# Row maxima of an attention block: transposed by 4-byte DMA loads instead of a TensorE matmul, and joined at the head of a step

## The chip, the cores and the metric

The kernel runs on one core of one Trainium2 chip. The metric is the device time of one execution in microseconds (us); the median of several runs counts. Five engines work side by side, each through its own queue in order: TensorE (PE, whose weight loads are listed apart as PEld), VectorE (DVE), ScalarE (ACT), GpSimd (POOL) and SyncE (SP), which issues most of the transfers. They meet through semaphores.

## The reference

A pre-normalized attention block with 32 heads of 16 dimensions over 2048 tokens, gated by the SiLU of a dense block with GELU:

```python
xn = _layernorm(x, axis=-1)                       # x: 1 x 2048 x 512
# attention, H = 32 heads, Dh = 16
scores = jnp.einsum("bhqd,bhkd->bhqk", q, k) * (Dh ** -0.5)
p = _softmax(scores, axis=-1)
o = jnp.einsum("bhqk,bhkd->bhqd", p, v)           # then @ wo
# dense block: 512 -> 1376 -> 512
h = _gelu(jnp.einsum("bsd,df->bsf", xn, w1) + b1)
g = _silu(jnp.einsum("bsf,fd->bsd", h, w2) + b2)
return x + s * g                                  # s: the attention's output
```

Everything is float32; the matmuls work on pairs of a rounded high part and a low rest. The weights are scaled up (factor 8), so the softmax needs its row maxima subtracted.

## The kernel before

**Units.** Attention is cut into 32 units. Unit `u` is a group of 4 heads (`g = u // 4`) and a chunk of 512 queries (`c = u % 4`). Each unit is gone through twice:
- *maxima* ("S"): 64 score tiles of 128 queries x 512 keys, which serve only to find each query's largest score. `s_mm` (L184) makes a tile in one of three banks, and `s_max` (L190) reduces it on DVE to two partial maxima per query in the tile `mx`. Two heads sit in the two 64-row halves of TensorE (`a` = 0, 1), two more behind each other (`p` = 0, 1).
- *attention*: in 16 steps of 128 keys each, four transposed score tiles of 128 keys x 512 queries ("T", `t_one`, L716), the exponential on ACT (L718), and the PV matmuls of the step before ("V", `pv_step`, L781).

**The maxima's way.** The subtraction is part of the T matmul: `QT[u]`, the queries of a unit, has two extra rows in each half (48 and 49) with the high and the low part of the negated maximum, against two rows of ones beside the keys. So the maxima, which arise one query to a partition, are needed as rows, one query to a column. Before, this goes in four parts. `s_end0` joins the 8 partial maxima of each query to `nm` (128 x 16, L248), behind the next S tile's reduction, and has POOL split them into `nmh` (L251, L252). `s_end1` transposes `nmh` by a matmul with the identity (L268), for two units at once up to unit 27 (`PAIRED`), into a bank of the S ring (stage one, and the last unit) or of the T ring. `s_end2` copies the result to `mh` (ACT in stage one, L276; DVE later, L278) and stores it in `mh_d` (L279). `load_mh` fetches two rows of a half in one transfer, two transfers a unit (L152). `later` counts ticks (four a step) until the transposition may be issued, and `need` is the first step at which `load_mh` may stand.

**Stages.** In stage one (to about 470 us) layer norm, the projections and the dense block run, and the first 576 S tiles (9 units, `LEAD`) are interleaved by `fill`. From then on come 512 attention steps, 16 a unit, their order written out by hand in `ORDER` and `AFTER`: with 3 S tiles (S, or X and Y for a tile in two halves), 4 T tiles and V a step until step 491, and with the output projection's half-array matmuls (`w_halves`, L905) afterwards. A short tail ends it. Small jobs (loads, divisions, gates) hang on steps in `todo`.

**Queues around the change.** SP issues, for each unit, the denominator's gather and four moves of the output (`o_move`, L801, L804), six query loads for attention (`load_qt`, L135), the maxima (`load_mh`), the denominators' store and broadcast load (`o_den`, L810, L813), and six query loads for the maxima of the unit after next (`load_qs`, L135, called at the end of `s_end0`). Near the end it also issues the gate's loads (`load_gx`, L837, L838). POOL issues the key loads of later groups (`load_k`, L110) and does the divisions (`o_div`, L819).

Of the kernel before, what the change touches and what calls it, by code (L numbers as in the profile page):

```python
# [8 lines left out]
F32 = mybir.dt.float32  # L9
# [7 lines left out]
P = 128  # L17
# [6 lines left out]
CH = 512  # L24
# [17 lines left out]
HC = CH // 2  # L42
PAIRED = 28
KB = 3
# [5 lines left out]
def fused(ctx: ExitStack, tc: tile.TileContext, x, wqk, wv, wo, w1, b1, w2, b2, out):  # L50
# [34 lines left out]

    QS, QT, MX, NM, MH = {}, {}, {}, {}, {}
    SYNC = mybir.DependencyInfo(mybir.DependencyClass.Sync, mybir.DependencyReason.DATA)
# [61 lines left out]
    def load_mh(u):  # L149
        assert u in sent  # L150
        for a in range(2):
            nc.sync.dma_start(QT[u][64 * a + 48:64 * a + 50].bitcast(F32), mh_d[u, :, a::2, :])  # L152

# [3 lines left out]
    later, ended, errands, sent = [], [], [], set()  # L157

    def units_of(u):
        return (u,) if u >= PAIRED else (u - u % 2, u - u % 2 + 1)  # L160

# [45 lines left out]

    jobs, whole, cut, put_off = [], [], [], []

    def s_op(op):  # L210
# [6 lines left out]
        elif op == "X":  # L217
# [4 lines left out]
            cut[2:] = [ps, pool, x]  # L222
            run_off()
        else:
# [9 lines left out]

    def run_off():
        while put_off:
            put_off.pop(0)()

    def s_end0(u):
        nm = qring.tile([P, GH * NCH], F32, name="nm")  # L240
        n = len(units_of(u))
        if u == units_of(u)[0]:
            NM[u] = qring.tile([P, 2, 2, GH * NCH], F32R, name="nmh")[:, :n]
        hl = NM[units_of(u)[0]][:, u % n]
        if u == units_of(u)[-1]:
            later.append([12 if "seen" in prog else 8, units_of(u)[0]])
        mx = MX.pop(u).rearrange("p a b c n -> p (a b) (c n)")
        nc.vector.tensor_reduce(nm, mx, axis=AX.X, op=OP.max, negate=True)  # L248

        def two():  # L250
            nc.gpsimd.tensor_copy(hl[:, 0], nm)  # L251
            nc.gpsimd.tensor_sub(hl[:, 1], nm, hl[:, 0].bitcast(F32))  # L252

        put_off.append(two)
        if "seen" in prog or u == NU - 1:
            run_off()
        del QS[u]
        if "seen" in prog:
            ask_qs(u + 2)
        else:  # L260
            load_qs(u + 2)

    prog = {}

    def s_end1(u):
        pm = s_tile()[0] if "seen" in prog or u == NU - 1 else t_tile()
        n = 2 * GH * NCH * len(units_of(u))
        nc.tensor.matmul(pm[:n, :P], NM.pop(u).rearrange("p u i a -> p (u i a)"), ident_r, start=True, stop=True)  # L268
        MH[u] = pm

    def s_end2(u):
        us = units_of(u)
        n = 2 * GH * NCH * len(us)
        mh = qring.tile([4 * GH * NCH, P], F32, name="mh", bufs=1)
        if "seen" in prog:
            nc.scalar.activation(mh[:n], MH.pop(u)[:n, :P], AF.Copy)  # L276
        else:
            nc.vector.tensor_copy(mh[:n], MH.pop(u)[:n, :P])  # L278
        nc.sync.dma_start(mh_d[us[0]:us[-1] + 1].rearrange("u i j (q s) -> (u i j q) s", s=P), mh[:n])  # L279
        sent.update(us)  # L280

# [277 lines left out]
    writer = {}  # L559
    s_when, put, row = [], [0], [0, 0]  # L560
    ndown = sum(1 for e in plan if e[0] == "down")
    ROWS = 12 * (4 * VQ + 2 * len(pairs)) + 6 * ndown - 10 + 2 * LEAD - 2 * (LEAD // 32) - FILL0

    def fill(a):
        due = FILL0 + put[0] + sum(made) * ROWS // (4 * LEAD)
        if sum(made) < 4 * LEAD and row[a] >= due and (made[0] <= made[1]) == (a == 0):
            taken()
            if later and later[0][0] <= 0:
                put[0] += 2
                u = later.pop(0)[1]  # L570
                s_end1(u)
                s_end2(u)
                return
            s_one(a)
            row[a] += 1
            tick()
# [357 lines left out]
    for u in range(NU):  # L934
# [116 lines left out]
```

## Time and profile before

| | us |
|---|---|
| median of 3 runs | 1572.92 (1572.62 to 1572.99) |
| the profiled execution | 1573.31 |
| its span | 1571.4 |
| S reductions on DVE, 2048 (L190) | 1298.8 busy |
| exponentials on ACT, 1533 + 515 (L718) | 826.0 + 310.9 busy |
| PV matmuls, 4096 (L781) | 545.3 busy |
| joining reductions, 32 (L248) | 8.8 busy |
| POOL's two parts of the split, 32 each (L251, L252) | 6.3 and 7.1 busy |

The profile is one execution, seen by the chip's profiler. A group row gives the line, the engine, the operation, tiles, count and durations (minimum / median / maximum in ns in the view of one tile or line). A timeline row gives start and length in us, engine, line, operation and, in square brackets, the idle time just before it with what ended it. A row of stages gives, for each engine, its busy time in the stage and its instructions. In the view of the transfers, a line of 40 digits is the mean busy share of the 16 DMA engines in 40 equal slices of the window, in tenths, and the row of a queue gives its packets, megabytes and the share of the 16 engines' time that they took. Tiles `slot`, `kt`, `qt` and `pst` are buffers that different stages share.

### The profile page before, as it was taken

What the parts mean: (1) busy time and instruction counts of PE and PEld (TensorE: products, weight loads), DVE (VectorE), ACT (ScalarE), POOL (GpSimd) and SP (SyncE); (2) the same over time, 40 slices, a digit from 0 to 9 for tenths busy, and PEclk for the clock granted to TensorE, in tenths of its full rate; (3) what the DMA queues carried; (4) which work ended last, traced back from release to release, by engine and by line L of the source; (5) the groups of instructions that cost most, each with busy time, mean ns of one, the idle gap of its engine ahead of it and who ended that gap; (6) DMA issues with size and microseconds to landing.
All of it is one profiled execution on the core that took longest, in us unless ns stands there. A gap on an engine that the chain in (4) does not pass through costs nothing.

```text
span 1571.4 us, 31849 instructions
## 1 busy us (share of the span) xinstructions
PE 1564.2 (100%) x12264; PEld 952.0 (61%) x12264; DVE 1397.1 (89%) x2290; ACT 1233.8 (79%) x2397; POOL 371.9 (24%) x394
## 2 busy tenths in 40 slices
PE   9999999999999999999999999999999999999998
PEld 7899999999994444444444444444444444444455
DVE  7599898989988999999999999999999999999834
ACT  4333333333339999999999999999999999999984
POOL 4145575766741001001100100100010000000143
PEclk9999999999999999999999999999999999999999
DMA  6626343454322114111511511321061111110163
GB/s 208 152 59 150 122 139 99 141 152 120 131 84 75 42 30 71 32 36 38 82 32 32 69 33 40 51 52 29 21 81 29 33 29 31 42 30 22 45 199 111
DMA packets 74648, 116.87 MB, mean 74 GB/s; under 512 B 23013, under 2 KB 24293, under 8 KB 73321
## 3 DMA queue, kind: packets, MB, share of 16 engines
q1 hardware_dynamic: 70748, 101.89, 24.1%
q0 software_dynamic: 3264, 12.35, 4.7%
q8 instruction: 97, 1.59, 0.4%
q10 hardware_dynamic: 484, 0.60, 0.1%
q14 instruction: 55, 0.44, 0.1%
HBM read 84.35 MB, written 25.97 MB: 70 GB/s over the span
## 4 chain that ended last, share of the span: by engine, by line
PE 98%; DVE 1%; ACT 0%; DMA 0%; issue 0%; DVEq 0%
PE pv L781 33%; PE pst L716 20%; PE ps L590 13%; PE ps L184 12%; PE pst L590 7%; PE ps L716 6%; PE pv L590 2%; PE ps L905 1%; PE ps L81 1%; PE ps L459 1%; PE pst L81 1%; DVE st L418 0%; PE pst L441 0%; DMA xt<-in_x 0%; PE pst L459 0%
## 5 line engine op out<-in xcount | busy, mean ns | idle before, releaser
L190 DVE TENSOR_REDUCE mx<-ps 128x2 f32<-128x512 f32 x2048 | 1298.8, 685 | 113.7 <-PE ps L184 45.5
L718 ACT ACTIVATE slot<-pst 128x512 f32<-128x512 f32 x1533 | 826.0, 603 | 14.0 <-PE pst L716 7.5
L781 PE MATMUL pv<-slot,vsb 128*32 128x512 f32 x4096 | 545.3, 605 | 0.3 <-DVE os L788 0.3
L716 PE MATMUL pst<-qt,kt 50*128 50x512 f32 x1149 | 380.3, 430 | 0.6 <-DVE gt L649 0.4
L184 PE MATMUL ps<-kt,slot 48*128 48x512 f32 (+1 forms) x1364 | 377.4, 367 | 0.0
L716 PEld LDWEIGHTS pst<-qt,kt 50*128 50x128 f32 x1149 | 191.6, 184 | 256.8 <-ACT slot L718 240.4
L718 ACT ACTIVATE slot<-ps 128x512 f32<-128x512 f32 x515 | 310.9, 604 | 1.9 <-PE ps L184 0.5
L184 PEld LDWEIGHTS ps<-kt,slot 48*128 48x128 f32 x1364 | 225.5, 184 | 40.3 <-DVE mx L190 35.2
L590 PE MATMUL ps<-slot,w1h 64*128 64x512 f32 x1088 | 217.8, 393 | 0.0
L184 PE MATMUL ps<-kt,qz 48*128 48x512 f32 x512 | 213.7, 417 | 0.0
L184 PE MATMUL ps<-slot,slot 48*128 48x512 f32 (+1 forms) x598 | 165.7, 366 | 0.0
L716 PE MATMUL ps<-qt,kt 50*128 50x512 f32 x387 | 160.0, 416 | 0.0
L590 PEld LDWEIGHTS ps<-slot,w1h 64*128 64x128 f32 x1088 | 154.4, 185 | 4.6
L590 PE MATMUL ps<-slot,w1l 64*128 64x512 f32 x544 | 142.0, 393 | 0.0
L781 PEld LDWEIGHTS pv<-slot,vsb 128*32 128x32 f32 x4096 | 80.7, 108 | 100.3 <-issue 92.3
L378 POOL TENSOR_TENSOR hl<-hg,hh 128x512 fp32r<-128x512 f32 x76 | 96.8, 1296 | 151.5 <-ACT hh L377 99.7
L371 ACT ACTIVATE hg<-ps,b_sb 128x512 f32<-128x512 f32 x44 | 27.8, 684 | 132.7 <-PE ps L590 116.9
L251 POOL CAST nmh<-nm 128x16 fp32r<-128x16 f32 x32 | 6.3, 196 | 489.1 <-DVE nm L248 466.6
L716 PE MATMUL pst<-qt,slot 50*128 50x512 f32 x384 | 111.3, 415 | 0.0
L184 PEld LDWEIGHTS ps<-slot,slot 48*128 48x128 f32 x598 | 98.8, 184 | 17.2 <-DVE mx L190 15.2
L184 PEld LDWEIGHTS ps<-kt,qz 48*128 48x128 f32 x512 | 93.7, 183 | 18.7
L716 PEld LDWEIGHTS ps<-qt,kt 50*128 50x128 f32 x387 | 71.1, 184 | 37.5 <-ACT slot L718 31.9
(165 smaller groups left out, 1715.7 us busy)
## 6 DMA issues: line engine op xcount, KB each, us to landing
raw<-in_w SPq DMA_DIRECT2D x88, 256.0 KB
qk_h<-hh SPq DMA_DIRECT2D x32, 256.0 KB
qk_l<-hl SPq DMA_DIRECT2D x32, 256.0 KB
qt<-qk_h SPq DMA_DIRECT2D x128, 64.0 KB
slot<-qk_h SPq DMA_DIRECT2D x92, 64.0 KB
g_d<-gt POOLq DMA_DIRECT2D x16, 256.0 KB, 3.5
qt<-qk_l SPq DMA_DIRECT2D x64, 64.0 KB
dn<-den_d SPq DMA_DIRECT2D x32, 128.0 KB
```

Of the source, the lines that this page charges most:

```text
L81: nc.tensor.matmul(ps, lhs[a], rhs[b], start=first and n == 0, stop=last and n == 2)
L184: return nc.tensor.matmul(ps[:, c0:c0 + w], QS[u][r, p, qi * P:(qi + 1) * P], kts[u // NCH % KB][p][r, k0:k0 + w], start=True, stop=True).ins
L190: nc.vector.tensor_reduce(MX[u][:, 2 * p:2 * p + 2, qi, ki][:, heads, parts], ps.rearrange("p (n c) -> p n c", c=HC), axis=AX.X, op=OP.max)
L251: nc.gpsimd.tensor_copy(hl[:, 0], nm)
L371: nc.scalar.activation(raw, ph.pop(u), AF.Gelu_apprx_tanh, bias=b1_sb[:, u[2]:u[2] + 1])
L378: nc.gpsimd.tensor_sub(hl, raw, hh.bitcast(F32))
L459: nc.tensor.matmul(pq["q", g, c], W1[g][i][:, k * P:(k + 1) * P], (xh, xl)[j][c][:, k], start=n == 0 and k == 0, stop=n == 2 and k == KT - 1)
L590: i = nc.tensor.matmul(ps, lhs[r], rhs[r], start=first, stop=last).ins
L716: nc.tensor.matmul(ps, kts[g % KB][p][r, k * P:(k + 1) * P], QT[u][r, p, :], start=True, stop=True)
L718: nc.scalar.activation(PT[u, k][:, 2 * p + a, :], ps, AF.Exp, scale=SCALE)
L781: nc.tensor.matmul(PV[u][32 * j:32 * j + 32, :], vsb[:, k, h:h + 32], PT[u, k][:, j, :], start=(k == 0), stop=(k == NT - 1))
L905: HALF[0] = nc.tensor.matmul(PW[i][0], OTS[i, k][x][r], (wo_h, wo_l)[y][r, k], start=k == 0 and side == 0 and n == 0, stop=k == KT - 1 and ...
```

## The change

The maxima are stored as POOL leaves them, 128 queries x 32 words, in a `mh_d` laid out that way, once a unit. `load_mh` makes four transfers a unit, one for each of the two rows of each half, and each picks 1024 single words out of `mh_d`, 128 bytes apart, and writes them as one row of 4 KB. The transposing matmul, its copy, the pairing of units and the deferred POOL parts (`put_off`) are gone.

The joining reduction stands at another place. In stage one it still follows the next S tile. In the attention steps it stands at the head of the step behind the one in which the unit's last S tile was reduced, ahead of that step's first tile; in the first three steps of a unit's 16 it is held back to the head of the fourth. POOL's two parts follow at once, and so does `load_qs`. The store may be issued 8 ticks later (4 for the last unit), and `need` is 7 steps behind the end of the unit's S tiles instead of 4 behind the end of the pair's. `fill` no longer gives a place to the transposition.

```diff
-    mh_d = dpool.tile([NG * NCH, 2, GH, CH], F32, name="mh_d")
+    mh_d = dpool.tile([NG * NCH, P, 2, 2, GH * NCH // 2], F32, name="mh_d")
...
     def load_mh(u):
         assert u in sent
         for a in range(2):
-            nc.sync.dma_start(QT[u][64 * a + 48:64 * a + 50].bitcast(F32), mh_d[u, :, a::2, :])
+            for i in range(2):
+                r = 64 * a + 48 + i
+                nc.sync.dma_start(QT[u][r:r + 1].bitcast(F32).rearrange("o p (q s) -> o (p q) s", s=P),
+                                  mh_d[u:u + 1, :, i, a].rearrange("o s j -> o j s"))
...
     def flush():
         while later and later[0][0] <= 0:
-            u = later.pop(0)[1]
-            run_off()
-            s_end1(u)
-            s_end2(u)
+            s_send(later.pop(0)[1])
...
         done[u] += 1
-        if ended:
-            s_end0(ended.pop())
         if done[u] == 64:
             ended.append(u)
-        if done[NU - 1] == 64:
-            s_end0(ended.pop())
...
-    def s_end0(u):
+    def s_end(u):
+        ended.remove(u)
+        NM[u] = qring.tile([P, 2, 2, GH * NCH // 2], F32R, name="nmh")
+        later.append([8 if u < NU - 1 else 4, u])
         nm = qring.tile([P, GH * NCH], F32, name="nm")
...
         mx = MX.pop(u).rearrange("p a b c n -> p (a b) (c n)")
         nc.vector.tensor_reduce(nm, mx, axis=AX.X, op=OP.max, negate=True)
-
-        def two():
-            nc.gpsimd.tensor_copy(hl[:, 0], nm)
-            nc.gpsimd.tensor_sub(hl[:, 1], nm, hl[:, 0].bitcast(F32))
-
-        put_off.append(two)
-        if "seen" in prog or u == NU - 1:
-            run_off()
+        nm = nm.rearrange("s (p a q) -> s a p q", p=2, a=2)
+        hi, lo = [NM[u][:, i].rearrange("s a (p q) -> s a p q", p=2) for i in range(2)]
+        nc.gpsimd.tensor_copy(hi, nm)
+        nc.gpsimd.tensor_sub(lo, nm, hi.bitcast(F32))
         del QS[u]
...
+    def s_send(u):
+        nc.sync.dma_start(mh_d[u], NM.pop(u).bitcast(F32))
+        sent.add(u)
...
-    def s_end1(u):
-        pm = s_tile()[0] if "seen" in prog or u == NU - 1 else t_tile()
-        n = 2 * GH * NCH * len(units_of(u))
-        nc.tensor.matmul(pm[:n, :P], NM.pop(u).rearrange("p u i a -> p (u i a)"), ident_r, start=True, stop=True)
-        MH[u] = pm
-
-    def s_end2(u):
...
-        nc.sync.dma_start(mh_d[us[0]:us[-1] + 1].rearrange("u i j (q s) -> (u i j q) s", s=P), mh[:n])
...
     def fill(a):
-        due = FILL0 + put[0] + sum(made) * ROWS // (4 * LEAD)
+        due = FILL0 + sum(made) * ROWS // (4 * LEAD)
...
-            if later and later[0][0] <= 0:
-                put[0] += 2
-                u = later.pop(0)[1]
-                s_end1(u)
-                s_end2(u)
-                return
+            flush()
+            ready = list(ended)
             s_one(a)
+            for u in ready:
+                s_end(u)
...
-            need = min(n for n in range(L) if due(n) >= 64 * (units_of(u)[-1] + 1)) + (4 if u < NU - 1 else 2)
+            need = min(n for n in range(L) if due(n) >= 64 * (u + 1)) + (7 if u < NU - 1 else 2)
...
         i = 0
+        for u in list(ended) if 2 < ka or u == NU - 1 else ():
+            s_end(u)
         order = ORDER[want] if n > 1 else ("TTTTV", "TTSTSVT")[n]
```

`ka` is the step's number within its unit of 16, `n` the step's number among the 512.

More of the change, by code (lines that the diff above doesn't have):

```diff
@@ L42 @@
 HC = CH // 2
-PAIRED = 28
 KB = 3
@@ L84, in mm3 @@
                 then()
-    QS, QT, MX, NM, MH = {}, {}, {}, {}, {}
+    QS, QT, MX, NM = {}, {}, {}, {}
     SYNC = mybir.DependencyInfo(mybir.DependencyClass.Sync, mybir.DependencyReason.DATA)
@@ L157, in fused @@
     later, ended, errands, sent = [], [], [], set()
-    def units_of(u):
-        return (u,) if u >= PAIRED else (u - u % 2, u - u % 2 + 1)
     def tick():
@@ L206, in s_one @@
         s_whole(heads[made[a] - 1], a)
-    jobs, whole, cut, put_off = [], [], [], []
+    jobs, whole, cut = [], [], []
     def s_op(op):
@@ L559, in fused @@
     writer = {}
-    s_when, put, row = [], [0], [0, 0]
+    s_when, row = [], [0, 0]
     ndown = sum(1 for e in plan if e[0] == "down")
-    ROWS = 12 * (4 * VQ + 2 * len(pairs)) + 6 * ndown - 10 + 2 * LEAD - 2 * (LEAD // 32) - FILL0
+    ROWS = 12 * (4 * VQ + 2 * len(pairs)) + 6 * ndown - 10 + 2 * LEAD - FILL0
     def fill(a):
-        due = FILL0 + put[0] + sum(made) * ROWS // (4 * LEAD)
+        due = FILL0 + sum(made) * ROWS // (4 * LEAD)
         if sum(made) < 4 * LEAD and row[a] >= due and (made[0] <= made[1]) == (a == 0):
             taken()
-            if later and later[0][0] <= 0:
-                put[0] += 2
-                u = later.pop(0)[1]
-                s_end1(u)
-                s_end2(u)
-                return
+            flush()
+            ready = list(ended)
             s_one(a)
+            for u in ready:
+                s_end(u)
             row[a] += 1
```

18 lines of the change are left out of this document (removed).

## The prediction

> **What bounds the kernel now.** I read the page first, then the busy time by stage, then the chain of waits, and last the timeline around the work that the change touches.
>
> ```profile
> span 1571.4 us, 31849 instructions
> PE 1564.2 (100%) x12264; PEld 952.0 (61%) x12264; DVE 1397.1 (89%) x2290; ACT 1233.8 (79%) x2397; POOL 371.9 (24%) x394
> ```
>
> ```profile
> 0.00:470.00 470.00, 467.62 (x3782) 424.52 (x3783) 403.48 (x666) 168.11 (x310) 256.96 (x235) 1.00 0.45 130
> 490.00:1486.00 996.00, 996.00 (x7761) 469.05 (x7757) 940.11 (x1547) 987.38 (x1937) 74.64 (x123) 1.00 0.20 40
> 1486.00:1571.40 85.40, 81.19 (x582) 47.28 (x581) 36.84 (x52) 59.53 (x116) 35.17 (x28) 1.00 0.46 153
> ```
>
> The columns after the length of the stage are PE, PEld, DVE, ACT, POOL, then TensorE's granted clock (1.00, full) and the DMA share. Stage one is TensorE's alone. In the long middle stage TensorE is busy throughout and ACT for 987.4 of 996 us, so 8.6 us of ACT idle is all that a better order there can win. In the last stage TensorE sets the pace again and ACT has room. POOL and the transfers are covered in all three: what they cost shows only if something reads a tile that has not landed.
>
> The chain of waits in the middle stage runs over the PV matmuls. These five are the first of units 2 to 6 (merged pieces, start and length):
>
> ```profile
> 543.12 1.05 PE pv L781 x8
> 576.06 1.07 PE pv L781 x8
> 608.85 1.04 PE pv L781 x8
> 641.96 1.06 PE pv L781 x8
> 674.73 1.05 PE pv L781 x8
> ```
>
> ```profile
> 565.80 0.28 DVE L248 TENSOR_REDUCE nm<-mx 128x16 f32<-128x128 f32 x1
> ...
> 611.13 0.28 DVE L248 TENSOR_REDUCE nm<-mx 128x16 f32<-128x128 f32 x1
> ...
> 614.20 0.27 PE L268 MATMUL pst<-ident_r,nmh 128*64 128x128 f32 x1
> ...
> 614.40 0.49 PE L716 MATMUL pst<-qt,kt 50*128 50x512 f32 x1
> ...
> 614.51 0.28 DVE L278 COPY mh<-pst 64x128 f32<-64x128 f32 x1
> ...
> 614.93 1.08 ACT L718 ACTIVATE slot<-pst 128x512 f32<-128x512 f32 x2 [0.32 <-PE ps L184]
> ...
> 653.59 0.28 DVE L248 TENSOR_REDUCE nm<-mx 128x16 f32<-128x128 f32 x1
> ```
>
> The units take 32.94, 32.79, 33.11 and 32.77 us. The second has neither a joining reduction (L248) nor a transposing matmul (L268). The first has one L248, at 565.80, and is 0.15 longer. The third has an L248 and an L268 and is 0.32 longer, so the matmul with its copy is 0.17. The fourth has an L248 at 653.59 and is no longer than the second: where this reduction stands decides whether it costs. Three tiles a step and 64 a unit (64 = 3 x 21 + 1) make the place rotate with period three. A unit that ends with a step's second tile has L248 behind the third, at the end of the step (653.59, free). One that ends with the third tile has it behind the next step's first tile (565.80, 0.15), and one that ends with the first tile behind the second (611.13, 0.15).
>
> **The change part by part.** *Removed: the transposing matmul, its copy, and a score bank for a moment.*
>
> ```profile
> L268 PE MATMUL ps<-ident_r,nmh x9: 247/274/276, 158.3 to 1490.1; 128*64 128x128 f32 x7, 128*32 128x128 f32 x2
> L268 PE MATMUL pst<-ident_r,nmh x9: 247/273/276, 614.2 to 1404.7; 128*64 128x128 f32 x7, 128*32 128x128 f32 x2
> ...
> L278 DVE COPY mh<-pst x9: 273/280/283, 614.5 to 1405.0; 64x128 f32<-64x128 f32 x7, 32x128 f32<-32x128 f32 x2
> L278 DVE COPY mh<-ps x5: 269/273/283, 523.8 to 1492.2; 64x128 f32<-64x128 f32 x3, 32x128 f32<-32x128 f32 x2
> ```
>
> There are 18 matmuls. By the copies 14 are in stages two and three and 4 in stage one, where ACT copies. From the matmul's start to the next one's it holds TensorE for 614.40 - 614.20 = 0.20 us.
> - Stage one: 4 x 0.20 = 0.8 us. The ends are nothing and 4 x 0.27, the whole matmul, = 1.1. The 4 copies leave an ACT that is busy for 168 of 470 us: nothing.
> - Middle stage: 13 x 0.17 = 2.2 us. The ends are nothing (ACT sets the step and catches up) and 13 x 0.32, ACT's idle time at 614.93, = 4.2. I take the unit lengths, since they are the path itself.
> - Last stage: one matmul, 0.2 us.
>
> *Moved: the joining reduction.* In the middle stage there are 22 (units 9 to 30); by the rotation 8 stand free now and 14 cost 0.15. The 7 like the one at 565.80 go one tile ahead, to the end of a step, which is where 653.59 is free: 7 x 0.15 = 1.05 us. The 7 like 611.13 end in the second step of a PV unit, where the change holds them back to the head of the fourth. There DVE may still be catching up from the copy of the unit's output, so I take half, 0.5. The ends for the move are a win of 14 x 0.15 = 2.1 and, if the new place blocks the first score tile of every step that it opens, a loss of 22 x 0.15 = 3.3. With it go the two POOL instructions (POOL is busy 75 of 996 us, so nothing; without that cover, behind one division, the store is 1.3 us later, which matters to unit 31 alone) and six SP transfers that fetch the queries of the unit after next. They are issued up to four tiles later, behind the query and maxima loads instead of ahead of them, and are read 64 tiles, some 43 us, later: nothing.
>
> ```profile
> L819 POOL TENSOR_TENSOR slot<-slot,dn x16: 1272/1282/1292, 531.5 to 1497.9; 64x512 f32<-64x512 f32 x16
> ```
>
> *Changed: the store.* 32 of 16 KB (128 rows of 128 bytes) instead of 18. Its nearest row is the store of the denominators, 128 rows of 64 bytes. The load behind that store waits for it, and follows 1.45 us later:
>
> ```profile
> 1481.43 0.34 SPq L810 DMA_DIRECT2D den_d<-dr  x1
> 1482.88 0.60 SPq L813 DMA_DIRECT2D dn<-den_d  x1
> ```
>
> The store now waits for POOL alone, instead of POOL, TensorE and DVE.
>
> *Added: the 4-byte loads.* Per unit, two loads of four 2 KB rows become four loads of 1024 separate words, 131,072 words in all. The trace of before has no such transfer. The nearest are two with 64-byte pieces, each alone in its half microsecond: the denominators' gather (4 rows on one side, 128 on the other) and the store above (128 on both sides).
>
> ```profile
> DMA  0000001122323131222231312232222000000000
> ...
> DMA packets 132, 0.01 MB, mean 16 GB/s; under 512 B 132, under 2 KB 132, under 8 KB 132
> ...
> q1 hardware_dynamic: 132, 0.01, 15.3%
> ```
>
> ```profile
> DMA packets 144, 0.01 MB, mean 17 GB/s; under 512 B 144, under 2 KB 144, under 8 KB 144
> ...
> q1 hardware_dynamic: 144, 0.01, 18.5%
> ```
>
> The first: 0.153 x 16 x 0.5 us / 132 = 9.3 ns a packet, with about 2 tenths of 16 engines (3 to 4) at work for 25 slices of 12.5 ns, 0.31 us; 128 pieces over 4 engines are 32 in 0.31 us, 9.8 ns each. The second: 10.3 ns. So a piece costs about 9.8 ns, and a transfer is spread over as many engines as the shorter side has rows. The new loads have 8 runs on the DRAM side, so I take 8 engines: 128 words each, 1.25 us a load, 5.0 us for four. The ends are one engine (the SBUF side is a single row): 40 us; and 16: 2.5 us. For a word the ends are 9.3 ns and the mean packet of SP's whole queue:
>
> ```profile
> q1 hardware_dynamic: 70748, 101.89, 24.1%
> ```
>
> 0.241 x 16 x 1571.4 / 70748 = 86 ns, at 1.4 KB a packet. I stay by the small packets, since size is what the two rows differ in most. What neither shows is words read from DRAM. One issue and the landing come on top:
>
> ```profile
> L152 SPq DMA_DIRECT2D qt<-mh_d x64: 603/660/742, 457.7 to 1494.7; - x64
> ```
>
> So the last word lands 0.66 + 5.0 + 1.45 = 7.1 us after the first load is issued. What time there is (first load issued, then the first score tile that reads it) is seen at a common unit, at unit 30 and at unit 31:
>
> ```profile
> 549.14 1.39 SPq L152 DMA_DIRECT2D qt<-mh_d  x2
> ...
> 572.95 0.50 PE L716 MATMUL pst<-qt,kt 50*128 50x512 f32 x1
> ```
>
> ```profile
> 1450.76 1.35 SPq L152 DMA_DIRECT2D qt<-mh_d  x2
> ...
> 1462.32 0.49 PE L716 MATMUL pst<-qt,kt 50*128 50x512 f32 x1
> ...
> 1483.53 0.45 SPq L837 DMA_DIRECT2D gx<-g_d  x1
> ...
> 1488.16 0.22 POOL L252 TENSOR_TENSOR nmh<-nm,nmh 128x16 fp32r<-128x16 f32 x1
> ...
> 1492.53 0.33 SPq L279 DMA_DIRECT2D mh_d<-mh  x1
> 1493.97 1.37 SPq L152 DMA_DIRECT2D qt<-mh_d  x2
> ...
> 1499.46 0.49 PE L716 MATMUL pst<-qt,kt 50*128 50x512 f32 x1
> ```
>
> A common unit has 23.8 us, unit 30 has 11.6, unit 31 has 5.5. But unit 31's store can leave when POOL ends at 1488.4, not at 1492.5, some of it behind four gate loads queued from 1483.53 on; with the 1.45 us its loads start near 1490.5 and have 9.0 us. So 7.1 us is hidden everywhere, and the loads cost nothing. Without that cover the PE, which takes its work in order, waits at the unit's first score tile, with PV and the maxima's matmuls behind it, and ACT and DVE wait for those. On SP the next denominator store and load, query loads and, at the end, gate loads queue behind the four; POOL's division and the last stage's gates on ACT wait for them. Both are late by 5 us at most, on engines busy for 75 of 996 and 59.5 of 85.4 us.
>
> **Sum:** 0.8 + 2.2 + 0.2 + 1.05 + 0.5 = 4.7 us off the profiled execution's 1573.3 (span 1571.4 and 1.9 around it): 1568.6. The median of the runs is 0.4 lower, 1572.9, so 1568 us.
>
> **The rivals.** *Late at the end.* A word costs 17 to 43 ns, and only units 31 and 30 wait. At 25 ns the loads need 12.8 + 2.1 = 14.9 us: unit 31 is late by 5.9, unit 30 by 3.3, and the time is 1568 + 9 = 1577; at 40 ns they need 22.6, late by 13.6 and 11.0: 1593. For it: no row reads words from DRAM, and SP's mean packet is 86 ns. Against it: both small-packet rows.
>
> *Every unit late (the slower side).* From (23.8 - 2.1) / 512 = 42 ns a word on, or with fewer engines at the price that I took, the usual window is too short and each unit start waits. At 50 ns: 27.7 us, 3.9 late x 27 units = 105, and 18.7 + 16.1 for the last two: 1568 + 140 = 1708. With one engine it would be beyond 2000. For it: four loads share one set of engines. Against it: the gather's use of 4 engines with 4 rows.
>
> [...]
>
> *Nothing won.* ACT, 99% busy, sets the middle stage, and the freed time returns as waits for ACT: 1572 to 1573. Against it: the unit lengths above follow the two instructions.
>
> **How the numbers follow.** Hidden loads: 0.58 (1568, own range 1565 to 1570). Late at the end: 0.17. Every unit late: 0.20. Nothing won: 0.05. This kernel's measurement tells about 0.2% (3.1 us) from no change. Hidden loads give faster, but for 0.03 of small gains: 0.55. These, nothing won, and 0.02 of the late end make 0.10 the same. The rest, 0.35, is slower. The range runs from the largest win (1.1 + 4.2 + 0.3 + 2.1 = 7.7 us, 1565) to the late end at 40 ns, 1593; every unit late is left out.
>
> **What would show it.** Right: four rows of word loads a unit, packets near 10 ns each, landed before the unit's first score tile; middle-stage units all near 32.8 us; 14 DVE copies and 18 PE matmuls gone. Wrong: TensorE idle at the first score tile of a unit with the load of the maxima as its releaser (at 30 and 31: the first rival; at most units: the second); units of 32.8 us but ACT as idle as before (the third); or a reduction at the head of a step with 0.15 us behind it.

## The result, and the profile after

| | before | after |
|---|---|---|
| median, us | 1572.97 (1572.62 to 1573.6, 6 runs) | 1683.26 (1677.92 to 1700.77, 6 runs) |
| ratio | | 1.0719, 95% interval 1.0671 to 1.0766 |
| profiled execution, its span | 1573.31, 1571.4 | 1681.43, 1679.7 |

The change makes the kernel 7% slower. From the page of the changed kernel, these lines answer to those of before (span, busy time, transfers, SP's queue, and the chain of work that ended last, by engine and by line):

```profile
span 1679.7 us, 31947 instructions
PE 1588.5 (95%) x12246; PEld 963.7 (57%) x12246; DVE 1396.9 (83%) x2276; ACT 1233.2 (73%) x2393; POOL 372.3 (22%) x394
...
DMA packets 209656, 116.88 MB, mean 70 GB/s; under 512 B 159300, under 2 KB 159556, under 8 KB 208328
...
q1 hardware_dynamic: 205756, 101.89, 48.3%
...
PE 76%; DMA 14%; SPq 6%; issue 2%; DVE 1%; POOL 1%; ACT 1%; ACTq 0%; POOLq 0%; DVEq 0%
PE pv L746 24%; DMA qt<-mh_d 12%; PE ps L555 11%; PE pst L681 10%; PE ps L681 9%; PE ps L180 9%; PE pst L555 6%; SPq L153 4%; PE pv L555 2%; PE ps L870 1%; SPq L134 1%; PE ps L426 1%; PE ps L80 1%; DMA mh_d<-nmh 1%; PE pv L459 1%
```

In the kernel before, the same row of the chain by engine was:

```profile
PE 98%; DVE 1%; ACT 0%; DMA 0%; issue 0%; DVEq 0%
```

18 matmuls are gone (12264 to 12246). SP's queue q1 moves the bytes that it moved before in 205756 packets instead of 70748, in 48.3% of the engines' time instead of 24.1%. Transfers now hold 14% of the chain, where they held nothing: the load of the maxima alone 12%, and its issue on SP (L153) another 4%.

The busy time by stage (after the length: PE, PEld, DVE, ACT, POOL, granted clock, DMA share), changed kernel:

```profile
0.00:470.00 470.00, 468.05 (x3795) 428.33 (x3797) 405.64 (x669) 168.96 (x310) 256.95 (x235) 1.00 0.48 130
490.00:1486.00 996.00, 943.53 (x7220) 442.10 (x7216) 875.77 (x1431) 920.28 (x1805) 72.00 (x119) 0.97 0.59 39
```

Stage one is as it was. In the same 996 us (the changed kernel's middle stage now lasts some 100 us longer) TensorE idles for 52 us and ACT for 76, and the transfers' share is 0.59 instead of 0.20.

One stalled unit, in the chain of waits (start, length; the end of unit 3, with the first score tile of unit 4 last):

```profile
589.54 0.42 SPq L134
...
592.96 0.74 SPq L153
593.75 1.02 SPq L153
594.81 1.22 SPq L153
596.08 22.59 DMA qt<-mh_d
618.66 0.14 issue
618.80 0.58 PE ps L681
```

SP issues the query loads (L134) and then four loads of the maxima (L153); the fourth is under way for 22.59 us, and the unit's first score matmul (L681) starts 0.14 us after it has landed. A unit that is not stalled shows the same in SP's queue (timeline, start and length of the issues):

```profile
1414.73 0.42 SPq L134 DMA_DIRECT2D qt<-qk_h  x1
1415.20 10.38 SPq L153 DMA_DIRECT2D qt<-mh_d  x4
1425.68 5.72 SPq L775 DMA_DIRECT2D den_d<-dr  x1
1436.47 0.58 SPq L778 DMA_DIRECT2D dn<-den_d  x1
```

The four issues take 10.38 us, where a query load takes 0.42; the next, the store of the denominators, takes 5.72, and the load that needs it goes out at 1436.47. The transfers in that time, first from 1415 to 1441 us, then for one microsecond after the fourth issue:

```profile
DMA  5616299999950004919000240010000000036557
...
DMA packets 4703, 0.69 MB, mean 26 GB/s; under 512 B 4394, under 2 KB 4394, under 8 KB 4701
```

```profile
DMA packets 412, 0.00 MB, mean 2 GB/s; under 512 B 412, under 2 KB 412, under 8 KB 412
## 3 DMA queue, kind: packets, MB, share of 16 engines
q1 hardware_dynamic: 412, 0.00, 97.4%
```

In that microsecond 412 packets of 4 bytes take 97.4% of the time of 16 engines, as the view counts it. (The first thousand words' packets took 9 ns each, most of those between 1419.0 and 1421.5 us 65 to 80. From 1422.3 to 1424.6 and from 1426.9 to 1429.6 no word's packet begins or ends: 16 of them, then 14, stay open, the longest for 3558 ns.)

The trace also has the transfers' landing events: a load of words has eight when it lands, the gather of the denominators four, the store of the maxima sixteen. No row of the page shows them, so I list them; the last of a load's events is when its reader may go (in units 4 and 17 the first score tile starts 0.1 us behind it). For the changed kernel, in us after a unit's first load was issued (its four loads; then the first score tile; and the length of the unit that this tile ends):

```
unit   last landing of loads 1 to 4     first score tile   length of the unit before
27     10.1   14.8   19.6   21.0        23.8               32.91  (free)
4                           25.7        25.8               40.68
17                          36.3        36.4               48.13  (POOL loads keys)
31                          22.2        22.6               55.86
all plain units              20.4 to 25.7; units 9, 13, 17, 21 (under key loads): 32.0 to 36.3
kernel before, two loads: 2.1 and 2.8
```

In unit 27 the first three loads land 4.7 to 4.8 us apart, the fourth 1.4 us behind the third. Over all four, less the 2.1 us that a load of before needs, (21.0 - 2.1) us / 4096 = 4.6 ns a word over all engines together.

### The profile page after: what moved, and what is told of

Read it like the earlier page. It is cut to its first block, busy times and chain, and to the rows that moved or that the text cites. A ratio compares the mean times of both kernels' runs of the same rounds, so it can differ in the third digit from the quotient of the medians.

```text
span 1679.7 us, 31947 instructions
## 1 busy us (share of the span) xinstructions
PE 1588.5 (95%) x12246; PEld 963.7 (57%) x12246; DVE 1396.9 (83%) x2276; ACT 1233.2 (73%) x2393; POOL 372.3 (22%) x394
## 3 DMA queue, kind: packets, MB, share of 16 engines
q1 hardware_dynamic: 205756, 101.89, 48.3%
## 4 chain that ended last, share of the span: by engine, by line
PE 76%; DMA 14%; SPq 6%; issue 2%; DVE 1%; POOL 1%; ACT 1%; ACTq 0%; POOLq 0%; DVEq 0%
PE pv L746 24%; DMA qt<-mh_d 12%; PE ps L555 11%; PE pst L681 10%; PE ps L681 9%; PE ps L180 9%; PE pst L555 6%; SPq L153 4%; PE pv L555 2%; PE ps L870 1%; SPq L134 1%; PE ps L426 1%; PE ps L80 1%; DMA mh_d<-nmh 1%; PE pv L459 1%
## 5 line engine op out<-in xcount | busy, mean ns | idle before, releaser
L186 DVE TENSOR_REDUCE mx<-ps 128x2 f32<-128x512 f32 x2048 | 1299.4, 686 | 190.3 <-PE ps L180 116.5
L683 ACT ACTIVATE slot<-pst 128x512 f32<-128x512 f32 x1533 | 803.6, 604 | 1.8 <-PE ps L681 1.2
L746 PE MATMUL pv<-slot,vsb 128*32 128x512 f32 x4096 | 556.6, 616 | 0.0
L180 PE MATMUL ps<-kt,slot 48*128 48x512 f32 (+1 forms) x1364 | 385.4, 372 | 0.0
L681 PE MATMUL pst<-qt,kt 50*128 50x512 f32 x1149 | 307.3, 408 | 0.1
L681 PEld LDWEIGHTS ps<-qt,kt 50*128 50x128 f32 x387 | 71.9, 187 | 353.2 <-ACT slot L683 287.5
L180 PEld LDWEIGHTS ps<-kt,slot 48*128 48x128 f32 x1364 | 230.0, 187 | 41.9 <-DVE mx L186 37.2
L681 PE MATMUL ps<-qt,kt 50*128 50x512 f32 x387 | 194.4, 505 | 62.3 <-DMA mh_d<-nmh 22.4
L681 PEld LDWEIGHTS pst<-qt,kt 50*128 50x128 f32 x1149 | 210.7, 188 | 19.3 <-DVE mx L186 1.3
L180 PEld LDWEIGHTS ps<-slot,slot 48*128 48x128 f32 x598 | 100.4, 187 | 17.5 <-DVE mx L186 15.9
L784 POOL TENSOR_TENSOR ot<-ot,dn 64x512 f32<-64x512 f32 x15 | 19.3, 1288 | 393.8 <-DMA dn<-den_d 284.5
L681 PE MATMUL pst<-qt,slot 50*128 50x512 f32 x384 | 101.5, 411 | 0.0
```

What stands on the lines that cost most here:

```text
L180: return nc.tensor.matmul(ps[:, c0:c0 + w], QS[u][r, p, qi * P:(qi + 1) * P], kts[u // NCH % KB][p][r, k0:k0 + w], start=True, stop=True).ins
L681: nc.tensor.matmul(ps, kts[g % KB][p][r, k * P:(k + 1) * P], QT[u][r, p, :], start=True, stop=True)
L683: nc.scalar.activation(PT[u, k][:, 2 * p + a, :], ps, AF.Exp, scale=SCALE)
L746: nc.tensor.matmul(PV[u][32 * j:32 * j + 32, :], vsb[:, k, h:h + 32], PT[u, k][:, j, :], start=(k == 0), stop=(k == NT - 1))
L784: eng.tensor_mul(ot[c][rs, g // 2], ot[c][rs, g // 2], DN.pop(u)[rs])
```

## The experiments

Ratios are to the kernel before, run on the same chip (1572.97 to 1573.43). A = the 4-byte words are the whole loss; B = something else in the change is.

**e1: no words.** One DVE instruction a unit turns the joined maxima in 32x32 blocks.

```diff
-        nc.sync.dma_start(mh_d[u], NM.pop(u).bitcast(F32))
+        nc.vector.transpose(turned, NM.pop(u)...rearrange("s i a j -> s (i a j)"))
+        nc.sync.dma_start(mh_d[u].rearrange("b i a j s -> (b i a j) s"), turned)
...
-                                  mh_d[u:u + 1, :, i, a].rearrange("o s j -> o j s"))
+                                  mh_d[u:u + 1, :, i, a].rearrange("o b j s -> o j b s"))
```

> The change with every 4-byte transfer taken out: the joined maxima are turned in 32x32 blocks by one DVE instruction a unit, stored as 128 rows of 128 bytes and loaded by the same four transfers in pieces of 128 bytes (128 pieces a unit in place of 4096). Everything else is as in the changed kernel, the reduction's new place too. Theory A (the 4-byte words are the whole loss): the nine stalls ahead of a unit's first score tile are gone, units at 32.8 us, and the sum of the prediction's other terms holds, 1566 to 1571 us. Theory B (part of the loss comes from the reduction's new place, or from four transfers where there were two): still over 1580 us, with TensorE waiting at the reduction's line.

Measured: 1567.44 us (5 runs), ratio 0.9963 (0.9949 to 0.9976): A, and 0.4% faster than the kernel before. From its page, the row of the turning instruction among the groups, the middle and last stage, and the first PV matmuls of units 2 to 6 in the chain:

```profile
span 1565.5 us, 31967 instructions
...
q1 hardware_dynamic: 78780, 101.89, 23.9%
```

```profile
L245 DVE STREAM_TRANSPOSE mh<-nmh 128x32 f32<-128x32 f32 x32 | 6.4, 201 | 0.0
```

```profile
488.20:1480.20 992.00, 992.00 (x7744) 468.54 (x7736) 938.12 (x1556) 987.54 (x1936) 74.62 (x123) 1.00 0.20 40
1480.20:1565.50 85.30, 81.11 (x583) 47.19 (x580) 36.97 (x52) 59.74 (x117) 35.16 (x28) 1.00 0.47 153
```

```profile
541.05 1.05 PE pv L748 x8
573.88 1.06 PE pv L748 x8
606.66 1.04 PE pv L748 x8
639.42 1.05 PE pv L748 x8
672.26 1.05 PE pv L748 x8
```

The units take 32.83, 32.78, 32.76 and 32.84 us, where before they took 32.94, 32.79, 33.11 and 32.77. TensorE has no idle time in the stage, and ACT only 4.5 of 992 us. In plain units each of the four loads lands 1.9 to 2.0 us after its issue. Without the words, and with the turning in their place, the rest of the change is a gain.

**e2: the reduction's new place alone**, in the kernel before (the load of the maxima may stand four steps later there).

```diff
-        if ended:
-            s_end0(ended.pop())
...
+        for u in list(ended) if 2 < ka else ():
+            s_end0(u)
```

> The kernel before with one part of the change, the joining reduction's new place (at the head of a step, held back in a PV unit's first three steps); the transposing matmuls and their copies stay. The prediction's step gives 1.05 + 0.5 us off: 1571.4 us, ends 1570.8 and 1576.2. If the new place were the loss, it would be over 1600.

Measured: 1572.84 us against 1573.43, ratio 0.9996 (0.9987 to 1.0005). The move costs nothing and wins nothing that can be told. Its units against those of before show why: of every three, one is some 0.15 us shorter and the next 0.1 longer (units 8, 9 and 10: -0.15, +0.11, 0.00); from the first to the last of them the sum is -0.05.

**e3: two of the four rows in words**, from a second store of the maxima as they lie.

```diff
+                if (a, i) in ((0, 0), (0, 1)):
+                    nc.sync.dma_start(... "o p (q s) -> o (p q) s" ..., mw_d[u:u + 1, :, i, a].rearrange("o s j -> o j s"))
+                    continue
```

> As the first of these kernels, with a second store of the maxima as they lie, and two of a unit's four loads, the first two, taken from it in 4-byte words (2048 words a unit), the other two in 128-byte pieces. Theory A1 (a word has a price of its own, about 4.9 ns over all engines): the loads are done 8 to 10 us after the first issue and the landing follows at 5 to 7, so 13 to 17 us of a window of 23.7; only the late units 29 to 31 and units under the key loads stall, 1575 to 1600 us. Theory A2 (the first load is cheap, 1 us, and only a load that follows on another's heels is dear): half of the four loads' time is not saved, but a third: SP is held some 4 us at the second load, and the time is 1580 to 1620.

Measured: 1593.49 us (1586.72 to 1594.89), ratio 1.0119 (1.0102 to 1.0137), which both theories allow. In plain units the words land some 11.4 and 13.1 us after the first issue, at the near end of A1's 13 to 17, and SP's two issues take 3.05 us in unit 3 and 1.82 in unit 25, short of A2's 4 at the second load. e5 parts the two. Time is lost only ahead of units 9, 13, 17 and 21 (key loads) and of 30 and 31, where the maxima come late.

**e4: the four loads apart in the program.**

```diff
-            at(max(16 * u - 14, need), load_mh, u)
+                for k in range(4):
+                    at(16 * u - 14 + 3 * k, load_mh, u, (k,))
```

> The changed kernel with all 4096 words a unit, but the four loads issued three steps (6.1 us) apart instead of back to back; the last is issued 10 us ahead of the first score tile. Units 29 to 31, whose maxima come late, keep the four together. Theory A1 (4.9 ns a word however issued): each load takes 5 us and lands 5 to 7 later, so the last one is just late or just in time, 1600 to 1650 us, and SP is held little. Theory A2 (dear only back to back): each load's words go in about 1 us, SP is not held, only units 29 to 31 stall, some 33 us: about 1600 us. Told apart by the words' packets in the trace: about 9 ns each in A2, 70 to 80 in A1.

Measured: 1762.96 us, ratio 1.1206 (1.1173 to 1.1239), worse than either theory said. SP's timeline in unit 3's turn:

```profile
561.20 2.90 SPq L155 DMA_DIRECT2D qt<-mh_d  x3
571.18 1.51 SPq L777 DMA_DIRECT2D den_d<-dr  x1
577.67 0.57 SPq L780 DMA_DIRECT2D dn<-den_d  x1
578.30 0.66 SPq L155 DMA_DIRECT2D qt<-mh_d  x1
```

SP is paced by what it waits for, not by the steps: three loads went together, and the fourth was caught behind the denominators' store and load, which themselves wait for the words ahead of them. So the loads were not spaced as intended, and the run does not tell what spacing gives; but the fourth load went alone. Most of its packets took 9 ns, SP was free at once, and yet it landed 6.6 us after its issue: 1024 words x 4.6 ns + 2.1 us, the landing of a load of before, are 6.8.

**e5: one row in words**, as e3 with `((0, 0),)`.

> As the kernel with two rows in words, but only the first of a unit's four loads goes in 4-byte words (1024 a unit); three go in 128-byte pieces. So far 0 rows gave 1567.4 us, two 1593.5, four 1683. Theory A1 (about 4.9 ns a word in all cases): 5 us of words a unit, a landing of 5 to 7 us: only unit 30 with its window of some 12 us is at the edge, 1568 to 1573 us, and the words last some 5 us in the trace. Theory A2 (cheap alone, dear on another's heels): the words go at 9 ns each in 1 to 2 us and SP is held for 0.75 us: 1567 to 1570 us. The time hardly parts the two; the packets do.

Measured: 1568.95 us, ratio 0.9977 (0.9968 to 0.9987). The packets look as A2 says: in unit 6 they took 9 ns each and were done 2.9 us after the issue, with SP held 0.74. The landing, 7.8 us after the issue (7.1 to 8.3 in plain units, 16.5 to 20.7 in the four under key loads), is A1's. So the packets' records end some 5 us before the load has landed; what goes on in those 5 us no trace shows. A2 is out: a lone load pays the price too, it is only not seen in its packets.

**e6: the words on the store's side.**

```diff
+        for a in range(2):
+            for i in range(2):
+                nc.sync.dma_start(mh_d[u, i, a].rearrange("j s -> s j"), nm[:, i, a])
```

> The changed kernel with the transposition on the other side: the maxima are stored in 4-byte words, four transfers of 1024 words from SBUF to DRAM, and loaded as four whole rows of 4 KB. A store has over 20 us until its load. If reading a word from DRAM is what is dear (B1): the stores go at some 9 ns a word, SP is not held, 1567 to 1570 us. If the price is in a word's transfer as such, whichever side it is scattered on (B2): the words hang as in the changed kernel, 16 us a unit, SP is held some 10 us at the fourth store; the loads themselves are quick, so only the units whose maxima come late (29 to 31) pay: 1580 to 1610 us.

Measured: 1926.51 us, ratio 1.2248 (1.2213 to 1.2282): B2 in kind, and far beyond its size. The four stores land 25.8 us after the first issue in unit 17 (23.4 in unit 14, 20.5 in unit 28). In stage one the weights' loads stand behind them in SP's queue: the first PV matmul comes at 597.4 us instead of 476.9, and the chain by line holds the weights (`raw<-in_w` 3%, `raw<-in_wqk` 2%) beside the stores (3%).

**e7: the words far apart in DRAM.**

```diff
-    mh_d = dpool.tile([NG * NCH, P, 2, 2, GH * NCH // 2], F32, name="mh_d")
+    mh_d = dpool.tile([NG * NCH, P, 1056], F32, name="mh_d")
```

> The changed kernel with 4224 bytes in DRAM from one query's maxima to the next instead of 128, so that a unit's 4096 words come from 540 KB and not from 16 KB; as many transfers, words and bytes. If words of one small region of DRAM get in each other's way (C1): the hang at the second load is gone, SP is held under 4 us, the time falls below 1600 us. If the price is of the words themselves (C2): the same stalls, 1670 to 1700 us. If lines far apart are dearer to read (C3): over 1720 us.

Measured: 1702.56 us, ratio 1.0824 (1.0802 to 1.0846), just above C2's range and below C3's. In unit 23 the loads land at 10.5, 15.2, 19.6 and 21.4 us, as in the changed kernel. Where in DRAM the words lie is not the cause.

**e8: everything three steps earlier.**

```diff
-            at(16 * u - 14, load_qt, u)
+            at(16 * u - 17, load_qt, u)
```

and the same for `load_mh`.

> The changed kernel with the query and maxima loads of a unit three steps (6.1 us) earlier in SP's program; nothing else. Theory A says that the four loads need some 23 us, or 30 to 36 under the key loads, against a window of 23.7. With 6 us more the units 3, 7, 8, 12, 16, 20 lose up to 6 us of their stall each (excess now 8, 6, 14, 12, 15, 11 us: 66 in all, some 33 left), while units 28 to 30 stay as they are, since their maxima are not ready sooner: about 1645 to 1655 us. If the stall did not hang on the window but on what the words do to other transfers (theory D: the denominators' chain behind them in SP's queue), the time would stay within 10 us of 1683 or rise.

Measured: 1873.13 us, ratio 1.1907 (1.1869 to 1.1946). The window theory alone falls, and theory D holds: the time rose. The chain and SP's timeline in one unit:

```profile
1433.73 0.88 PE pv L746 x5
1434.61 12.22 DMA dr<-os
1446.86 0.25 DVE dr L774
1447.11 0.55 DVE mx L186
1447.71 1.17 PE ps L180 x2
```

```profile
1422.93 11.58 SPq L153 DMA_DIRECT2D qt<-mh_d  x4
1434.61 4.90 SPq L766 DMA_DIRECT2D dr<-os  x1
```

The score tiles have their maxima in time now. But the gather of the denominators (L766) stands behind the words, lands 12.22 us after its issue (in the changed kernel 1.9 to 3.3), and DVE, which takes its reciprocal (L774), stands still until then with the score maxima of S (L186) behind it; TensorE has no free bank and waits. Moving the loads moves the stall.

**e9 to e11: where the price lies.** These are e1 with one more store as in e3. e9 adds four transfers of words into 8 partitions each, e10 the same into DRAM (nobody reads either); e11 fetches the two low rows in 8-byte pieces (they then stand at the wrong queries).

```diff
+                nc.sync.dma_start(dm[32 * (2 * a + i):32 * (2 * a + i) + 8], mw_d[u, :, i, a].rearrange("s j -> j s"))
...
+                nc.sync.dma_start(dd_d[u, i, a], mw_d[u, :, i, a].rearrange("s j -> j s"))
...
+                mw_d[u:u + 1, :, i, a].rearrange("o s (k w) -> o k s w", w=2)
```

> The first of these kernels (turned by DVE, 1567.4 us) with four extra transfers a unit behind the four loads, whose result nobody reads: the same 4096 words, from a copy of the maxima that lies as in the changed kernel, but each transfer's 1024 words go into 8 partitions of 128 words instead of one row of 1024. What is asked is when they land. In the changed kernel four loads in words land one about every 5 us, 21 us in all (first issue to last landing), one alone 6.4 to 7.7 us after its issue, although its packets are done in 2. Theory W (a partition takes a word only every 4.9 ns): with 8 partitions they land within 2 to 4 us of their issue. Theory V (4.9 ns for any word into SBUF): 20 us again, and the denominators' transfers behind them are late; then 1575 to 1650 us.

> The same with the extra four transfers of 1024 words going from the copy of the maxima to another place in DRAM, four rows of 4 KB, so that SBUF has no part in them; nobody reads the result. Theory W or V (the price is on SBUF's side): they land within some 3 us. Theory R (it is on the side of DRAM's reads, a word at a time): 20 us again. The stores in words, which took 20 us as well, went to DRAM, so I expect at least as much here: 20 to 30 us and 1580 to 1700 us.

> As the kernel with two rows in words, but the two rows are the low halves of both head pairs and they go in pieces of 8 bytes (512 pieces each, 1024 a unit in place of 2048, as many bytes); the low halves then stand at the wrong queries, which changes the result by rounding only. Two rows in words took 12 to 13 us from the first issue to the landing. Theory P (the price is by the piece, 4.9 ns): 5 us less, landing some 7 to 8 us after the first issue, 1567 to 1570 us. Theory Q (by the byte): 12 to 13 us again and about 1593 us.

Measured: e9 1573.28 us, ratio 1.000 (0.9989 to 1.0012); e10 2182.69, ratio 1.3872 (1.3832 to 1.3913); e11 1568.07, ratio 0.9969 (0.9953 to 0.9985). The landings, in us from the first issue in words to the last landing of each transfer, in one plain unit each (e6: unit 17):

```
changed kernel  4 x 1024 words, each into one row of SBUF     10.1  14.8  19.6  21.0
e9              4 x 1024 words, each into 8 partitions         4.6   6.1   8.1   8.9
e10             4 x 1024 words, each into a row of DRAM       12.2  22.2  27.9  36.6
e6              4 x 1024 words from SBUF, scattered in DRAM   12.5  24.7  24.9  25.8
e3              2 x 1024 words into rows of SBUF              11.4  13.1
e11             2 x 512 pieces of 8 bytes into rows of SBUF    5.4   6.2
e5, e4's last   1 x 1024 words into a row of SBUF              6.0 to 8.3
e1              4 x 32 pieces of 128 bytes                     1.9   2.7   3.4   4.2
```

e11 against e3: half the pieces with the same bytes take half the time, and e1 brings the bytes of the changed kernel into the same rows in 128 pieces and 4.2 us, so the price is by the piece (P). Nor does it look like one engine's: a load of e11 has four landing events where one of e3 has eight, so if each is an engine's, which no run shows, both give an engine 128 pieces a load, and e11 still takes half. The words of e9 and e10 are read like those of the changed kernel and differ in the destination (and stand behind four small loads). The same reads take 8.9 us into 8 partitions and 21.0 into one row: there the price is on the writing side (R falls). e10's time is far beyond the 1580 to 1700 us expected of it, and its 36.6 us are not DRAM's writing alone, as far as this shows, since e6 writes as many words to DRAM, from SBUF, in 20.5 to 25.8. W was too bold: 8 partitions are 2.4 times as fast as one row, not 5 to 10 times. What it is in the destination that makes this factor of 2.4, no run shows.

**e12: two queues**, the second head pair's two loads on POOL's.

```diff
-                nc.sync.dma_start(QT[u][r:r + 1]...
+                (nc.gpsimd if a else nc.sync).dma_start(QT[u][r:r + 1]...
```

> The changed kernel with all 4096 words a unit, but the two loads of the second head pair go through POOL's queue instead of SP's. So far four loads in words on SP's queue land 21 to 25 us after the first issue, one more every 5 us, and SP is held some 10 us. Theory X (the 5 ns are a limit of one queue): SP's two and POOL's two run side by side, each pair landed after 10 to 13 us, SP is not held beyond 4 us, and only the late units and those under the key loads pay: 1580 to 1620 us. Theory Y (the limit is behind the queues, where the words of all queues meet): the last landing stays at 20 us or more after the first issue, whatever queue; SP is held less, so the denominators' transfers go sooner: 1630 to 1690 us. POOL has to wait for the query buffer in its own order, which may delay the divisions and key loads in its queue and add to either.

Measured: 1622.89 us (two runs), ratio 1.0317 (1.0173 to 1.0462), between X and Y; whether it is more than 2% slower than before, two runs leave open. In unit 29, where both queues began together (1431.29 us), the four landed after 11.2, 16.9, 18.4 and 18.6 us; in the seven units where they began within some 3 us of each other, the last landed after 18.6 to 25.9, hardly sooner than on one queue (20.4 to 25.7). POOL's pair alone took some 12.8, SP's pair alone 13.5. The limit is behind the queues (Y); against the changed kernel, the gain is that SP is held for 1.8 us instead of 10, and that POOL's pair was issued 10 to 16 us ahead of SP's in 22 of 32 units.

## Why the prediction was wrong

**The step that failed: 9.8 ns a word, on 8 engines side by side (5.0 us for four loads, 7.1 with issue and landing).** The packets do take 9 ns at first (the first thousand of unit 27), and eight landing events a load fit the 8 engines; but the loads do not land as if 8 engines wrote the words side by side. By the landings a word takes 4.6 ns for all engines together: (21.0 - 2.1) / 512 = 37 ns a word in the prediction's count, up to 41 in the units that land after 23. The four loads need 21 to 25 us where I had 7.1, against the usual window of 23.8. My two small-packet rows were of 64-byte pieces, and the time that packets take does not tell when a load has landed (in e5 done 2.9 us after the issue, landed at 7.8). That is the first rival's price, at the top of its 17 to 43 ns; it gave 1593 at 40 ns, and 1683 came. The rivals split at 42 ns as if each unit stood alone; the measured time lies between the two.

**What neither rival had.** Against e1, the changed kernel's execution is 114.1 us longer, by unit lengths: 9.1 ahead of the first PV unit (unit 0, whose first score tile waits 6.41 us for its maxima, at 479.19); 51.8 in the four units ahead of 9, 13, 17 and 21; 33.5 in the three ahead of 29, 30 and 31 (the first rival had 25 for two of these); 13.6 ahead of 4 and 8; 6.1 in all others. Unit 0 could have been seen: in the trace of before its window is 15.4 us (457.70 to 473.07), not 23.8, and I took units 30 and 31 alone as short. The largest part is where POOL loads keys. Its timeline, then SP's, and TensorE's first score tile of unit 17:

```profile
1057.50 1.08 POOL L109 DMA_DIRECT2D kt<-qk_h  x2 [0.28 <-issue]
1058.58 0.50 POOL L109 DMA_DIRECT2D kt<-qk_l  x1
1059.07 0.99 POOL L109 DMA_DIRECT2D kt<-qk_h  x2
1060.05 0.50 POOL L109 DMA_DIRECT2D kt<-qk_l  x1
```

```profile
1059.17 23.90 SPq L153 DMA_DIRECT2D qt<-mh_d  x4
```

```profile
1095.59 0.76 PE L681 MATMUL ps<-qt,kt 50*128 50x512 f32 x1 [12.67 <-DMA mh_d<-nmh]
```

Six key loads are issued at the same time as the words; SP is held for 23.90 us and the last load lands at 1095.46, 0.13 us ahead of the matmul that had waited for 12.67. (The row names a store of the maxima as its releaser. That one belongs to a later unit and lands from 1095.55 to 1097.10, so the load is the releaser.) The prediction priced the loads alone in the queues and did not look for what POOL's queue does in that window. It is not the words alone that the key loads hold back. In e1 the same four loads in long pieces land 13.0 to 17.5 us after their first issue in units 9, 13, 17 and 21, against 4.0 to 4.6 in the others (6.7 in unit 5), while the key loads' queue takes most of the engines' time (e1, unit 17, from 1006.50 to 1023.00 us):

```profile
q0 software_dynamic: 288, 1.57, 74.3%
q1 hardware_dynamic: 522, 0.50, 25.3%
```

In e1 that fits into windows of 22.8 to 23.6 us and costs nothing; in the changed kernel the words come on top, 14 to 20 us more, and it does not fit. Before the change, too, the loads of units 13 and 17 landed 10.5 and 6.8 us after their first issue instead of some 3, so the prediction's trace held a sign of it.

The rest is SP's queue: the words hold it, the denominators' chain behind them is late, and so are the next unit's loads. Unit 4's were issued 36.3 us after unit 3's (556.69, 592.96), in a rhythm of 32.8. I had named what is queued behind the reduction, and not what is queued behind the loads.

A stall also leaves TensorE slow for a while. These rows show the changed kernel behind the stall that ends at 618.8 us, by granted clock (the last figure but two), and the PV matmuls there:

```profile
618.80:622.80 4.00, 4.00 (x17) 1.80 (x19) 1.53 (x3) 2.06 (x4) 0.20 (x1) 0.50 0.10 35
622.80:626.80 4.00, 4.00 (x28) 1.96 (x30) 2.93 (x5) 2.68 (x6) 2.57 (x4) 0.71 0.46 81
```

```profile
620.63 1.86 PE pv L746 x8
624.28 1.43 PE pv L746 x8
626.74 0.99 PE pv L746 x8
```

The two steps from 620.63 take 6.1 us instead of 4.1. Behind the other eight stalls from unit 4 on, the first two steps lose 0.9 to 2.8 us in the same way, some 15 us in all nine. The granted clock is down to 0.50 for 3.4 to 17.1 us at each stall, and stays at 1.00 until the end in the traces of before and e1. No rival counted it.

**The removed joins: right in sign, too small.** e1 has the whole sum without the words: its span is 6.0 us shorter (1571.45 to 1565.47), where I had 4.7, and that includes its turning on DVE. Up to the first PV matmul it is 1.9 (I had 0.8, end 1.1); why so much, no run shows. The 13 units of the middle stage that hold a join are 3.5 shorter together, 0.27 each, and e2 gives none of it to the new place in sum: nearer to 0.32, ACT's idle time, than to the 0.17 that I took from unit lengths. The unit with the last stage's join gave the expected 0.2.

**The moved reduction: wrong.** 1.05 + 0.5 us were expected; e2 shows 0.05 in these units, and 0.6 in the medians, which is within the noise. The units that have it at a step's end are 0.15 shorter, as 653.59 suggested, but the unit behind them is longer by 0.1. The loss of 3.3, the other end, did not come either.

**What is shown and what is not.** Shown: without words the loss is gone and the forecast's time is there (e1); the price is by the piece (e1, e11), whatever the place in DRAM (e7), and for words into SBUF on the writing side (e9); and both the late landing and SP's held queue stall TensorE (the changed kernel's chain, e8). That the limit lies behind the queues rests on the seven units of e12 in which both queues began within 3 us. Not shown: which part of the writing side takes 4.6 ns a word, what makes e10 slower than e6, and how the key loads hold back what is issued beside them, since no kernel tried the words without them. "Nothing won" is refuted by e1.

## What to carry to other kernels

Here the price of small pieces showed in their landing, not in the time of their packets (2.9 us of packets, 7.8 to the landing in e5): measure one such load from issue to landing before costing it, and count pieces, not bytes (half the pieces with the same bytes landed after 6.2 us instead of 13.1, e11 against e3). Read the window of every unit, the first and those beside other loads too, and not only of a common one. Then look for what stands behind it in its queue and for what other queues do in that window: here four loads in words landed after 20.4 to 25.7 us in plain units and 32.0 to 36.3 under the key loads. To turn a small tile, a transposition in 32x32 blocks on an engine with room (0.20 us of DVE a unit here) with long pieces beat both a matmul with its copy and a scattering transfer here (1567.44 us against 1572.97 and 1683.26).

## What the runs showed of the hardware that was not expected

- A lone load of 1024 words is taken at 9 ns a packet, done 2.9 us after its issue (e5), and lands 6.0 to 8.3 us after it. In the changed kernel, where more words follow, the packets show it (unit 27): most between 1419.0 and 1421.5 us take 65 to 80 ns each, and in two stretches, of 2.3 and 2.7 us, 14 to 16 packets stay open and none ends. The store of the denominators behind them, issued at 1425.68, landed at 1436.42, 0.2 us after the last load: 10.74 us, where the one of 1415.67 in the kernel before took 1.42.
- The issuing engine is held too: SP for 10.38 us on the changed kernel's four loads in unit 27, for 23.90 under key loads in unit 17.
- Words from DRAM to DRAM took longer than from DRAM into rows of SBUF: 36.6 us for 4096 (8.9 ns each, e10) against 21.0 (5.1, the changed kernel).
- Beside key loads, loads in longer pieces are late too: four in 128-byte pieces land after 13.0 to 17.5 us there, after 4.0 to 4.6 elsewhere (6.7 in unit 5, e1).
- Two words a piece halved the price (two loads landed after 6.2 us in e11, 13.1 in e3), and loads in pieces of 128 bytes land in 1.9 to 2.0 us in plain units (e1), like a load of before (2.1).
